# Routing statements of a three-stage kernel with one operand in a PSUM bank, rounds joined at their ends, and a new table of times for the order of its second phase

## The chip, the core and the metric

The kernel runs on one core of a Trainium2 chip. A core has five engines that work side by side, each through its own list of instructions in order: TensorE (matrix products; PE in the views, PEld for its weight loads), VectorE (DVE), ScalarE (ACT), GpSimd (POOL) and SyncE (SP, which here only issues transfers). They wait for each other through semaphores. Tiles lie in SBUF, results of TensorE in PSUM, which has eight banks; VectorE and ScalarE can reach PSUM too. The metric is the time of one execution on the device in microseconds.

## What is computed

Attention with decaying weights, then a dense layer pair, then a routed layer with eight experts. The last part is what the change touches:

```
logits = x @ w_gate                      # 4608 tokens, 8 experts
order  = argsort(-logits.flatten())      # all (token, expert) pairs, best first
for (tok, e) in order:
    if assigned[tok] >= 0 or counts[e] >= 576: continue
    assigned[tok] = e; counts[e] += 1
for e in range(8):
    h = maximum(x[assigned == e] @ w1[e], 0)      # 512 -> 1024
    out[assigned == e] = h @ w2[e]                # 1024 -> 512
```

Every expert gets exactly 576 tokens. The products are made in pieces of high and low part (three matmuls in place of one) for accuracy.

## The kernel before

`phase_ab` does the attention and the dense pair and ends at about 1042 us of the span; `phase_c` (from L711) does the routing and the experts. The greedy choice is made in eight rounds, one for each expert that fills up. `route(r)` is one round: it masks the logits (`v`), takes each token's best (`m`, `mt`), turns it into a sortable key (`n1`, `key`, `hi`), marks what each token proposes (`e0`, `m8`, `P`), and then finds the threshold at which the first expert is full by a search of six steps (two halves of three, `STEPS`). A step compares all keys with 32 or 64 thresholds (`cmp_`, 128x1152 or 128x2304 results), counts with TensorE (L865 or L869 into `pa`), masks (`ca`, L873), sums with TensorE again (L884, L885 into `pd`), and reduces to the new threshold (`dm`, `tr`, `pi`). Then come the counts (`GG`, L909), the expert that is full (`mx`, `ei`), the tokens' places (`X`, L932 and L933; `pos`, `zi`, `zl`, `zh`), the list of its tokens (`A`, `b1`, `R`, L962; `im`, `ix`, L973; `idx`, L976), and last the masks for the next round (`se`, `epen`, `tpen`, `own`, `rem`, L981 to L987). So a round is one long chain that goes to and fro between VectorE and TensorE. In rounds below `FAST` (0 and 1) GpSimd makes the differences `D` for the later steps (L833), so that their compare has one tile and a scalar.

Expert `r` needs `EI[r]` (which weights to load; SyncE) and `IDX[r]` (which rows of x to gather; GpSimd). `experts(r)` is TensorE's main work: 192 matmuls of 128x288 (L1090, first layer) and 112 of 128x512 (L1121, second layer). ScalarE and VectorE take each result over as `hh` and `hl` (L1099, L1103: three VectorE instructions for one f, a set in what follows). `split_w` makes high and low part of each weight tile, the low one on GpSimd (`w1l`, `w2l`, L1008), and `tokens` transposes the gathered rows (L1044) and splits them (`xh`, `xl`, L1046, L1047).

Each engine's order is fixed when the program is written. `route`, `weights` and `tokens` are generators that yield planned durations (`Y_TR`, `Y_Z` and the others, in us); every few matmuls `experts` calls `tick`, which moves a planned clock by `TK1` or `TK2` and lets each generator whose time has come (yield times `YS`) write its next instructions behind the matmuls written so far. A yield that is too short places a routing matmul on TensorE before its operand is ready, and as TensorE works in order, all matmuls behind it wait. Before the first expert, rounds 0 and a part of 1 run alone: `run(...)` writes round 0, a row of `WARM2` matmuls (L1147), `LEAD` = 8 pieces of round 1, then the transposes for expert 0.

Of the kernel before, what the change touches and what calls it, by code (L numbers as in the profile page):

```python
# [9 lines left out]
F32 = mybir.dt.float32  # L10
F32R = mybir.dt.float32r
# [689 lines left out]
RZ = 0.8
YS = 1.0
# [12 lines left out]
def phase_c(tc, ctx, w1, w2, rtf, rti, rth, rtb, x2d, L, out):  # L715
# [7 lines left out]
    psR = ctx.enter_context(tc.tile_pool(name="psR", bufs=2, space=PSUM))  # L723
# [41 lines left out]
    nc.gpsimd.memset(sc, 0.0)  # L765
    EI, IDX = {}, {}

    def route(r):
# [27 lines left out]
        GG = rt([128, NCOL, 2, E], BF16, "GG")
        gg = rt([128, NCOL, 2], BF16, "gg")
        if r < E - 1:

            n1 = rt([128, NCOL], I32, "n1")  # L800
            key = rt([128, NCOL], I32, "key")
            hi = rt([128, NCOL], I32, "hi")
            lo = rt([128, NCOL], I32, "lo")
            hs = rt([128, NCOL], F32, "hs")
            lf = rt([128, NCOL], F32, "lf")
            mb = mt.bitcast(I32)
            V.tensor_scalar(n1, mb, c31, c80, op0=OP.arith_shift_right, op1=OP.bitwise_or)
# [4 lines left out]
            for half in range(2):
# [6 lines left out]
                D = [None] * 3  # L819
                for s, (shift, J) in enumerate(STEPS):  # L820
                    io = F[f"s{s}"]
                    cmp_ = rt([128, NCOL, J], BF16, f"cmp{J}")
                    if s == 0:
                        V.tensor_tensor(cmp_, bc(src, 2, J), bc(io, 1, NCOL), op=OP.is_ge)
                        if fast:
                            if not half:
                                src = rt([128, NCOL], F32, "hf")
                                nc.gpsimd.tensor_copy(out=src, in_=hi)
                            for k in (1, 2):
                                D[k] = fp.tile([128, KC, CAP], F32R, tag=("xh", "xl")[k - 1], name=f"D{k}", bufs=2)  # L830
                                D[k] = D[k].rearrange("p k t -> p (k t)")[:, :NCOL * STEPS[k][1]].bitcast(F32)
                                D[k] = D[k].rearrange("p (c j) -> p c j", c=NCOL)
                                nc.gpsimd.tensor_tensor(D[k], bc(src, 2, STEPS[k][1]), bc(F[f"s{k}"], 1, NCOL),  # L833
                                                        op=OP.subtract)
                        if not half:
                            yield 1.3
# [3 lines left out]
                            V.tensor_scalar(rn[:1], rem[:1], -1.0, None, op0=OP.mult)  # L840
                            V.tensor_copy(out=rz[:1, 1, :], in_=rn[:1])
                    else:
                        if fast:
                            if s == 1:
                                V.tensor_scalar(cmp_, D[s], pi, None, op0=OP.is_ge)
                            else:
                                V.tensor_scalar(cmp_, D[s], T, pi, op0=OP.subtract, op1=OP.is_ge)
                        else:
                            thr = rt([128, J], F32, f"thr{J}")
                            if s == 1:  # L850
                                V.tensor_scalar(thr, io, pi, None, op0=OP.add)
                            else:
                                V.tensor_scalar(thr, io, T, pi, op0=OP.add, op1=OP.add)
                            V.tensor_tensor(cmp_, bc(src, 2, J), bc(thr, 1, NCOL), op=OP.is_ge)
# [378 lines left out]
```

## Time and profile before

| | |
|---|---|
| median of 3 runs | 1649.44 us (1648.26 to 1654.27) |
| the profiled execution | 1648.73 us, span 1647.0 us |
| dense phase, until about | 1042 us |
| routing before the first expert matmul | 1046.6 to about 1110 us |
| experts 0 to 5, each with a round of routing beside it | 1110 to 1533 us, 68 to 76 us each |
| experts 6 and 7, no routing left | 1533 to 1638 us |
| busy over the span | TensorE 92%, VectorE 73%, ScalarE 46%, GpSimd 37% |

How to read it: the busy shares are means over phases with different limits. In the dense phase TensorE has hardly a pause. In the expert phase it is again the engine with the most work, so what matters there is each wait of TensorE and what released it. In the stretch before the first expert nothing runs but the routing chain, so every instruction of it counts.

### The profile page before, as it was taken

Reading aid. Unit: us, or ns where it says so; the run is one execution under the profiler, and the core shown is the slowest. Engines: PE = TensorE matmul, PEld = TensorE weight load, DVE = VectorE, ACT = ScalarE, POOL = GpSimd, SP = SyncE. Lnnn points to the kernel's source line nnn. Section 1 sums busy time; section 2 is a strip of 40 time slices with the busy share of each in tenths; the row PEclk is TensorE's granted clock in tenths of the full one; section 3 lists DMA queues with packets and bytes.
Section 4 is the critical chain, followed back from the end, with each engine's and each line's share of the span. In section 5 each row is a group of like instructions: output and inputs, shape, how many; then the busy total and the mean of one; then the engine's idle time right before and its main releaser. Section 6 shows DMA issues by size and latency. Waiting matters only on the chain.

```text
span 1647.0 us, 25621 instructions
## 1 busy us (share of the span) xinstructions
PE 1508.3 (92%) x9204; PEld 1306.3 (79%) x9204; DVE 1205.0 (73%) x2743; ACT 759.4 (46%) x1581; POOL 611.3 (37%) x500
## 2 busy tenths in 40 slices
PE   6989999999999999999999999438889898898997
PEld 4778878888888888888888889328678687786986
DVE  6989965878777777777777778676777777778410
ACT  4667764555555545464545565222332232222421
POOL 4546631212121212121212122454554635546442
PEclk8889999999999999999999999759999999999999
DMA  7422221120201111111111000131332313323511
GB/s 264 153 80 77 78 104 65 39 77 21 76 29 69 39 58 39 58 47 51 58 39 58 22 20 1 34 102 44 121 115 74 125 56 121 109 74 101 172 61 36
DMA packets 48607, 122.34 MB, mean 74 GB/s; under 512 B 6624, under 2 KB 13536, under 8 KB 48224
## 3 DMA queue, kind: packets, MB, share of 16 engines
q1 hardware_dynamic: 41184, 99.80, 18.1%
q0 software_dynamic: 6144, 19.93, 3.8%
q8 instruction: 72, 1.18, 0.3%
q10 hardware_dynamic: 1152, 0.98, 0.2%
q14 instruction: 55, 0.45, 0.1%
HBM read 101.81 MB, written 18.87 MB: 73 GB/s over the span
## 4 chain that ended last, share of the span: by engine, by line
PE 72%; DVE 21%; issue 3%; ACT 2%; DMA 2%; POOL 0%; SPq 0%; ACTq 0%; POOLq 0%; DVEq 0%
PE h L394 21%; PE x L457 21%; PE ff L1090 11%; PE ff L1121 7%; PE ps L292 2%; PE ps L339 2%; PE ps L285 2%; PE ps L344 2%; DVE t L418 1%; PE tp L1044 1%; DVE work L204 1%; DVE P L794 1%; DVE t L424 1%; DVE e L790 1%; DVE work L203 1%
## 5 line engine op out<-in xcount | busy, mean ns | idle before, releaser
L438 POOL TENSOR_TENSOR gl<-t,gh 128x384 fp32r<-128x384 f32 x192 | 203.7, 1061 | 664.6 <-ACT gh L435 612.0
L394 PE MATMUL h<-xh,w0h 128*128 128x384 f32 x704 | 240.8, 342 | 3.7 <-DVE t L424 3.6
L394 PE MATMUL h<-xh,w0l 128*128 128x384 f32 x704 | 240.3, 341 | 0.0
L457 PE MATMUL x<-w1h,gh 128*128 128x512 f32 x576 | 236.3, 410 | 2.4 <-ACT gh L435 2.4
L404 ACT ACTIVATE S<-h 128x384 f32<-128x384 f32 x192 | 93.6, 487 | 307.0 <-PE h L394 306.6
L418 DVE SCALAR_TENSOR_TENSOR t<-t,S 128x384 f32<-128x384 f32 x192 | 114.9, 599 | 162.1 <-ACT t L407 161.1
L457 PE MATMUL x<-w1l,gh 128*128 128x512 f32 x576 | 230.0, 399 | 0.0
L457 PE MATMUL x<-w1h,gl 128*128 128x512 f32 x576 | 218.9, 398 | 0.4 <-POOL gl L438 0.4
L495 DVE SCALAR_TENSOR_TENSOR junk<-x2r,wg 128x512 f32<-128x512 f32 x240 | 164.2, 684 | 4.7
L394 PE MATMUL h<-xl,w0h 128*128 128x384 f32 x704 | 153.2, 340 | 0.0
L394 PEld LDWEIGHTS h<-xh,w0h 128*128 128x128 f32 x704 | 133.7, 190 | 13.4 <-DVE t L424 5.7
L1008 POOL TENSOR_TENSOR w2l<-ws,w2h 128x512 fp32r<-128x512 f32 x64 | 91.2, 1424 | 137.0 <-ACT w2h L1007 123.6
L394 PEld LDWEIGHTS h<-xh,w0l 128*128 128x128 f32 x704 | 133.6, 190 | 7.3
L1121 PE MATMUL ff<-w2h,hh 128*128 128x512 f32 x320 | 134.2, 419 | 0.0
L1121 PE MATMUL ff<-w2l,hh 128*128 128x512 f32 (+1 forms) x320 | 132.5, 414 | 0.0
L457 PEld LDWEIGHTS x<-w1h,gl 128*128 128x128 f32 x576 | 108.7, 189 | 27.4 <-POOL gl L438 1.5
L424 DVE COPY_PREDICATED t<-m,h 128x384 f32<-128x384 uint16 x192 | 114.8, 598 | 20.4 <-ACT m L413 0.7
L407 ACT ACTIVATE t<-S,bias 128x384 f32<-128x384 f32 x192 | 118.3, 616 | 19.2 <-POOL gl L438 3.3
L394 PEld LDWEIGHTS h<-xl,w0h 128*128 128x128 f32 x704 | 126.9, 189 | 0.0
L457 PEld LDWEIGHTS x<-w1h,gh 128*128 128x128 f32 x576 | 109.8, 191 | 20.9 <-ACT gh L435 3.0
L457 PEld LDWEIGHTS x<-w1l,gh 128*128 128x128 f32 x576 | 109.8, 191 | 18.0
L420 DVE TENSOR_TENSOR t<-t,h 128x384 f32<-128x384 f32 x192 | 106.3, 554 | 18.6 <-ACT T L410 0.9
(208 smaller groups left out, 3176.5 us busy)
## 6 DMA issues: line engine op xcount, KB each, us to landing
ws<-in_w SPq DMA_DIRECT2D x128, 256.0 KB, 4.1
ain<-in_qkv SPq DMA_DIRECT2D x36, 768.0 KB, 4.2
wst<-in_wio SPq DMA_DIRECT2D x32, 512.0 KB, 3.5
x2d<-x2r SPq DMA_DIRECT2D x33, 256.0 KB, 2.0
w1h<-in_qkv SPq DMA_DIRECT2D x12, 192.0 KB, 3.6
w1l<-in_qkv SPq DMA_DIRECT2D x12, 192.0 KB, 3.6
w0h<-in_qkv SPq DMA_DIRECT2D x12, 192.0 KB, 3.6
w0l<-in_qkv SPq DMA_DIRECT2D x12, 192.0 KB, 3.8
```

The costliest lines, as they stand in the source:

```text
L394: nc.tensor.matmul(h[:, :TB], w[0][f][:, hp, :], x, start=i == 0, stop=i == 11)
L404: nc.scalar.activation(S, h, AF.Square, scale=KSC)
L407: nc.scalar.activation(AT[s][2], AT[s][1], AF.Square, bias=bias[:, 0:1])
L418: nc.vector.scalar_tensor_tensor(t, t, PA - PB * PB / 4, S, op0=OP.add, op1=OP.mult)
L420: nc.vector.tensor_tensor(t, t, h, op=OP.mult)
L424: nc.vector.copy_predicated(t, m.bitcast(U16), h)
L438: nc.gpsimd.tensor_tensor(G[s][1], TT.pop(s), G[s][0].bitcast(F32), op=OP.subtract)
L457: nc.tensor.matmul(X2[n][i], g[:, i * 128:i * 128 + 128], w, start=(f == 0 and g is gh and w is wh), stop=(f == NF - 1 and g is gl))
L495: nc.vector.scalar_tensor_tensor(j, r, 1.0, wg[e // 4][:, e % 4, :], op0=OP.mult, op1=OP.mult, accum_out=L[:, c, e:e + 1])
L1008: nc.gpsimd.tensor_tensor(l, s, h.bitcast(F32), op=OP.subtract)
L1090: nc.tensor.matmul(ps[u], w[:, k, :], x[:, k, 288 * u:288 * u + 288], start=i == 0, stop=i == 11)
L1121: nc.tensor.matmul(o, h, w, start=f == 0 and i == 0, stop=f == 7 and i == len(prods) - 1, skip_group_check=t == 4)
```

## The change

Seven things are changed, all in `phase_c`.

1. A PSUM bank `st` (pool `psS`) is set aside and cut into pieces `SB[...]`. It holds `epen`, `own`, `rem`, copies of the small tables (`w8`, `s0`, `col`, `c`), and the results `m`, `key`, `n1`, `e0`, `hs`, `thr`, `gg`, `pos`, `eq`, `pa`, `zi`, `zl`, `zh`. With it every VectorE statement of `route` with two tiles has at most one of them in SBUF, and most statements with one tile read or write the bank. Nine small VectorE instructions fill it before round 0 (three of the fills stood on GpSimd).
2. The bank comes from `psR`, which has one rotating buffer in place of two; `pt` and `pc` share it.
3. `FAST` is 1: round 1 has no `D`. In round 0 `D` is made for the third step of each half alone; the second step compares against thresholds.
4. The ends of rounds overlap: `se`, `epen` and the next `v` are made behind the `X` matmuls; `tpen`, `own`, `rem` while TensorE makes the list (L962, now L989); `m`, `mt` of the next round before `idx`; the next key and first compare right behind `idx`.
5. `R[:, :, 1, :]` is made on ScalarE in all rounds (L958 is gone), and `b1` stands before `A`.
6. The yields have new values, and `YS` is 0.87 for all three generators; `RZ` is gone.
7. `LEAD` is still 8, but with fewer yields at a round's start these 8 pieces reach further: two whole steps of round 1 and the third compare.

```
-FAST = 2
+FAST = 1
-Y_TR = 1.35 ... Y_GG = 2.2, Y_X = 1.75, Y_R = 2.0, Y_Z = 1.6, Y_H = 0.35, Y_CA = 1.3, Y_IX = 1.65, RZ = 0.8, YS = 1.0
+Y_TR, Y_CA, Y_H, Y_GG, Y_X, Y_Z, Y_R, Y_IX = 2.0, 0.85, 0.5, 2.9, 2.7, 3.6, 1.3, 2.1
+YS = 0.87
...
-    psR = ctx.enter_context(tc.tile_pool(name="psR", bufs=2, space=PSUM))
+    psR = ctx.enter_context(tc.tile_pool(name="psR", bufs=1, space=PSUM))
+    psS = ctx.enter_context(tc.tile_pool(name="psS", bufs=1, space=PSUM))
...
+    bank = psS.tile([128, 512], F32, tag="st", name="st")
+    SB = {"epen": 8, "w8": 8, "s0": 32, "m": 36, "key": 36, "col": 36, "own": 36, "rem": 8, "c": 3, "e0": 288}
...
+    def best(r):
+        V.tensor_reduce(SB["m"], VN[r], axis=AX.X, op=OP.max)
+        MT[r] = rt([128, NCOL], F32, "mt")
+        V.tensor_tensor(MT[r], SB["m"], tpen, op=OP.min)
+    def keys(r):
+        n1 = SB["n1"].bitcast(I32)
+        HI[r] = rt([128, NCOL], I32, "hi")
+        mb = MT[r].bitcast(I32)
+        V.tensor_scalar(n1, mb, c31, c80, op0=OP.arith_shift_right, op1=OP.bitwise_or)
+        V.tensor_tensor(key, mb, n1, op=OP.bitwise_xor)
+        V.tensor_scalar(HI[r], key, c16, cff, op0=OP.arith_shift_right, op1=OP.bitwise_and)
+        compare0(r, HI[r])
+    def compare0(r, src):
+        CM[r] = rt([128, NCOL, 32], BF16, "cmp32")
+        V.tensor_tensor(CM[r], bc(src, 2, 32), bc(SB["s0"], 1, NCOL), op=OP.is_ge)
...
-            V.tensor_tensor(e0, v, bc(m, 2, E), op=OP.is_equal)
+            V.tensor_tensor(q0, v, bc(m, 2, E), op=OP.is_equal)
-            V.tensor_tensor(e0, e0, bc(F["w8"], 1, NCOL), op=OP.mult)
+            V.tensor_tensor(e0, q0, bc(SB["w8"], 1, NCOL), op=OP.mult)
...
         nc.tensor.matmul(pt[:, 72:], B["ones"], X72, start=True, stop=True)
         nc.tensor.matmul(pt[:, :72], B["tri"], X72, start=True, stop=True)
+        if r < E - 1:
+            V.tensor_scalar(se, SB["w8"], mx, None, op0=OP.is_equal)
+            V.scalar_tensor_tensor(epen, se, -2 * BIG, epen, op0=OP.mult, op1=OP.add)
+            V.tensor_tensor(VN[r + 1], L, bc(epen, 1, NCOL), op=OP.min)
...
+        V.tensor_tensor(b1, bc(zh, 2, 20), bc(F["i20"], 1, NCOL), op=OP.is_equal)
+        nc.scalar.activation(R[:, :, 1, :], b1, AF.Copy, scale=F["p"])
+        yield Y_Z
         V.tensor_tensor(A, bc(zl, 2, 32), bc(F["i32"], 1, NCOL), op=OP.is_equal)
-        yield 1.3
-        V.tensor_tensor(b1, bc(zh, 2, 20), bc(F["i20"], 1, NCOL), op=OP.is_equal)
-        yield 0.9
-        V.tensor_tensor(R[:, :, 0, :], b1, bc(F["col"], 2, 20), op=OP.mult)
+        yield 1.4
+        V.tensor_tensor(R[:, :, 0, :], b1, bc(SB["col"], 2, 20), op=OP.mult)
-            V.tensor_scalar(R[:, :, 1, :], b1, F["p"], None, op0=OP.mult)
```

In VectorE's order the change shows at three places. First, from the list of round 1's tokens to the proposals of round 2. Before (the last twelve here end at `mt`; the eight instructions from `n` to `P` follow):

```order
L976 TENSOR_REDUCE idx<-rt 128x5
L981 TENSOR_SCALAR se<-tf,mx 128x8
L982 SCALAR_TENSOR_TENSOR epen<-se,epen 128x8
L983 TENSOR_TENSOR tk<-gg,vd 128x36
L984 SCALAR_TENSOR_TENSOR tpen<-tk,tpen 128x36
L985 TENSOR_TENSOR m_10766<-m_10766,gg 128x36
L986 TENSOR_TENSOR own<-own,m_10766 128x36
L987 TENSOR_TENSOR rem<-rem,nn 128x8
L1129 TENSOR_TENSOR o<-ff,o 64x512
L780 TENSOR_TENSOR v<-L,epen 128x288
L782 TENSOR_REDUCE m<-v 128x36
L784 TENSOR_TENSOR mt<-m,tpen 128x36
```

After, from `m` to `P` (`st` is any piece of the bank):

```order
L788 TENSOR_REDUCE st<-v 128x36
L790 TENSOR_TENSOR mt<-st,tpen 128x36
L1012 TENSOR_REDUCE idx<-rt 128x5
L797 TENSOR_SCALAR st<-mt,ti 128x36
L798 TENSOR_TENSOR st<-mt,st 128x36
L799 TENSOR_SCALAR hi<-st,ti 128x36
L804 TENSOR_TENSOR cmp_11467<-hi,st 128x1152
L822 TENSOR_TENSOR q_11495<-v,st 128x288
L1158 TENSOR_TENSOR o<-ff,o 64x512
L824 TENSOR_TENSOR st<-q_11495,st 128x288
L826 TENSOR_REDUCE m_11496<-st 128x36
L828 TENSOR_TENSOR P<-st,m_11496 128x288
```

What stood between `idx` and `mt` has gone to places further ahead. On TensorE 40 matmuls of the second layer lie between L973 and the next L865 before, and 27 between L1007 and L892 after.

Second, from the places of the tokens to `R` in a later round, before (`hl` and `hh` are the sets of the expert):

```order
L944 TENSOR_SCALAR zl<-zi,ti 128x36
L945 TENSOR_SCALAR zh<-zi,ti 128x36
L1103 SCALAR_TENSOR_TENSOR hl<-ff,hh 128x288
L1103 SCALAR_TENSOR_TENSOR hl<-ff,hh 128x224
L1103 SCALAR_TENSOR_TENSOR hh<-ff,hh 128x64
L950 TENSOR_TENSOR A<-zl,tf 128x1152
L952 TENSOR_TENSOR b_13095<-zh,tf 128x720
L954 TENSOR_TENSOR R<-b_13095,tf 128x36x20
L958 TENSOR_SCALAR R<-b_13095,tf 128x36x20
```

And after:

```order
L976 TENSOR_SCALAR st<-st,ti 128x36
L980 TENSOR_TENSOR b_12145<-st,tf 128x720
L1132 SCALAR_TENSOR_TENSOR hl<-ff,hh 128x288
L1132 SCALAR_TENSOR_TENSOR hl<-ff,hh 128x224
L1132 SCALAR_TENSOR_TENSOR hh<-ff,hh 128x64
L983 TENSOR_TENSOR A<-st,tf 128x1152
L1132 SCALAR_TENSOR_TENSOR hl<-ff,hh 128x288
L1132 SCALAR_TENSOR_TENSOR hl<-ff,hh 128x224
L1132 SCALAR_TENSOR_TENSOR hh<-ff,hh 128x64
L985 TENSOR_TENSOR R<-b_12145,st 128x36x20
```

`A` and `b1` have changed places, `R` has one instruction fewer on VectorE, and there is one set more between them. On TensorE 4 matmuls of L1090 and 28 of L1121 lie between L933 and L962 before, and 50 of L1119 (the old L1090) between L958 and L989 after, in rounds 4 to 6; 14 and 19, or 36 and 8, in rounds 1 and 2.

Third, ahead of the first expert: the `xl` of expert 0, before,

```order
L838 TENSOR_SCALAR lo<-key,ti 128x36
L839 TENSOR_SCALAR hs<-hi 128x36
L840 TENSOR_SCALAR rn<-rem 1x8
L841 COPY rz<-rn 1x8
L1047 TENSOR_TENSOR xl_10800<-tp,xh_10799 128x4x128 x4
L1047 TENSOR_TENSOR xl_10800<-tp,xh_10799 128x4x64
L873 TENSOR_TENSOR ca<-rt,tf 128x32
```

and after:

```order
L922 SCALAR_TENSOR_TENSOR tr_10825,pi<-tr_10825,st 128x31
L884 TENSOR_SCALAR st<-tf,pi 128x64
L886 COPY T<-st 128x1
L887 TENSOR_TENSOR cmp_10832<-hi,st 128x2304
L1076 TENSOR_TENSOR xl_10838<-tp,xh_10837 128x4x128 x4
L1076 TENSOR_TENSOR xl_10838<-tp,xh_10837 128x4x64
L900 TENSOR_TENSOR ca<-rt,tf 128x32
```

They stand behind two more steps and a compare of round 1, and on TensorE the transposes stand behind those two steps' matmuls.

## Rows read from the trace of the kernel before

**Rows 1.** Windows view: us, busy us of five engines, granted TensorE clock, DMA.

```profile
core 0: us, PE busy (x) PEld busy (x) DVE busy (x) ACT busy (x) POOL busy (x), PEclk, DMA share, GB/s
1110.00:1186.00 76.00, 64.74 (x478) 55.86 (x477) 54.22 (x132) 20.66 (x43) 40.75 (x28) 0.92 0.27 85
1186.00:1533.00 347.00, 311.73 (x2150) 267.71 (x2150) 267.98 (x634) 100.39 (x210) 177.14 (x130) 0.95 0.32 102
...
1143.00:1165.00 22.00, 18.46 (x101) 14.46 (x100) 18.64 (x44) 7.59 (x14) 12.70 (x11) 1.00 0.48 156
```

**Rows 2.** Waits view, TensorE, expert phase (1110 to 1638 us): total, times, longest.

```profile
PE rt L962 <- DVE R L958: 16.9, 5, 3.6
PE rt L865 <- DVE P L794: 16.4, 5, 5.2
PE rt L932 <- DVE ei L927: 5.2, 7, 1.2
PE rt L909 <- DVE GG L905: 3.0, 2, 2.3
PE rt L962 <- ACT R L956: 1.6, 1, 1.6
PE ff L1090 <- DVE hl L1103: 1.4, 1, 1.4
PE rt L865 <- DVE cmp L845: 0.9, 1, 0.9
```

**Rows 3.** Tile view, readers of table tf: duration in ns, min/median/max.

```profile
L873 DVE TENSOR_TENSOR ca<-rt,tf x42: 168/191/193, 1057.1 to 1486.9; 128x32 f16<-128x32 f32 x42
...
L950 DVE TENSOR_TENSOR A<-zl,tf x8: 1341/1884/2461, 1084.9 to 1525.8; 128x1152 bf16<-128x1152 int32 x8
```

**Rows 4.** Timeline, VectorE and GpSimd, round 5: start, us, engine, instruction.

```profile
1425.67 1.29 POOL L1008 TENSOR_TENSOR w2l<-ws,w2h 128x512 fp32r<-128x512 f32 x1 [3.31 <-ACT w2h L1007]
...
1425.77 1.23 DVE L944 TENSOR_SCALAR zl<-zi,ti 128x36 int32<-128x36 int32 x1
...
1427.06 0.74 DVE L1103 SCALAR_TENSOR_TENSOR hl<-ff,hh 128x288 fp32r<-128x288 f32 x2
...
1427.86 2.42 DVE L950 TENSOR_TENSOR A<-zl,tf 128x1152 bf16<-128x1152 int32 x1
```

**Rows 5.** Timeline, the same engines, ahead of the first expert.

```profile
1097.99 7.73 DVE L838 TENSOR_SCALAR lo<-key,ti 128x36 int32<-128x36 int32 x1
...
1105.95 6.22 POOL L833 TENSOR_TENSOR D<-hf,tf 128x1152 f32<-128x1152 f32 x2
1106.01 1.27 DVE L1047 TENSOR_TENSOR xl<-tp,xh 128x512 fp32r<-128x512 f32 x2
```

**Rows 6.** Timeline, VectorE in round 0, on its own on the chip's critical chain.

```profile
1050.07 2.30 DVE L790 TENSOR_TENSOR e<-e,tf 128x288 f32<-128x288 f32 x1
...
1052.89 3.74 DVE L794 TENSOR_TENSOR P<-e,m 128x288 bf16<-128x288 f32 x1
...
1068.90 4.50 DVE L845 TENSOR_SCALAR cmp<-D,pi 128x1152 bf16<-128x1152 f32 x1
...
1083.11 0.30 DVE L936 TENSOR_TENSOR_SCAN sc<-one,rt 128x72 f32<-128x72 f32 x1 [0.27 <-PE rt L932]
...
1087.06 0.91 DVE L954 TENSOR_TENSOR R<-b,tf 128x720 bf16<-128x720 bf16 x1
...
1091.37 0.17 DVE L976 TENSOR_REDUCE idx<-rt 128x5 int32<-128x10 f32 x1 [0.34 <-PE rt L973]
```

**Rows 7.** Timeline, VectorE, round 1 with GpSimd at rest.

```profile
1093.75 0.52 DVE L807 TENSOR_SCALAR n<-mt,ti 128x36 int32<-128x36 int32 x1
...
1097.61 0.46 DVE L794 TENSOR_TENSOR P<-e,m 128x288 bf16<-128x288 f32 x1
```

**Rows 8.** Chain that ended last, the last two experts: start, us, what.

```profile
1561.11 25.49 PE ff L1121 x112
1586.60 25.58 PE ff L1090 x192
```

More of the change, by code (lines that the diff above doesn't have):

```diff
@@ L746, in ps_r @@
         return psR.tile([128, 512], F32, tag="rt", name="rt")[:, :n]
+    bank = psS.tile([128, 512], F32, tag="st", name="st")
+    SB = {"epen": 8, "w8": 8, "s0": 32, "m": 36, "key": 36, "col": 36, "own": 36, "rem": 8, "c": 3, "e0": 288}
+    at = 0
+    for k, n in SB.items():
+        SB[k] = bank[:, at:at + n]
+        at += n
+    at = 0
+    for k, n in {"thr": 64, "hs": 36, "gg": 72, "pos": 72, "eq": 36}.items():
+        SB[k] = SB["e0"][:, at:at + n]
+        at += n
+    SB["n1"] = SB["thr"][:, :36]
+    SB["zi"], SB["pa"] = SB["thr"][:, :36], SB["hs"]
+    SB["zl"], SB["zh"] = SB["eq"], SB["pos"][:, 36:]
+    epen, own, rem = SB["epen"], SB["own"], SB["rem"]
     tpen = kp.tile([128, NCOL], F32, name="tpen")
-    epen = kp.tile([128, E], F32, name="epen")
-    rem = kp.tile([128, E], F32, name="rem")
-    own = kp.tile([128, NCOL], F32, name="own")
     rn = kp.tile([128, E], F16, name="rn")
@@ L765, in phase_c @@
     nc.gpsimd.memset(sc, 0.0)
-    EI, IDX = {}, {}
+    V.memset(epen, BIG)
+    V.memset(own, 0.0)
+    V.memset(rem, float(CAP))
+    for k in ("w8", "s0", "col"):
+        V.tensor_copy(out=SB[k], in_=F[k])
+    for i, (shift, _) in enumerate(STEPS):
+        V.memset(SB["c"][:, i:i + 1], float(1 << shift))
+    EI, IDX = {}, {}
+    VN, MT, HI, CM = {0: L}, {}, {}, {}
+    key = SB["key"].bitcast(I32)
+    def best(r):
[13 more added lines that the diff above has]
+        V.tensor_tensor(CM[r], bc(src, 2, 32), bc(SB["s0"], 1, NCOL), op=OP.is_ge)
     def route(r):
         fast = r < FAST
-        v = rt([128, NCOL, E], F32, "v")
-        m = rt([128, NCOL], F32, "m")
-        e0 = rt([128, NCOL, E], F32, "e0")
+        q0 = rt([128, NCOL, E], F32, "q0")
+        e0 = SB["e0"].rearrange("p (c e) -> p c e", e=E)
         m8 = rt([128, NCOL], F32, "m8")
@@ L839, in route @@
                             V.tensor_scalar(hs, hi, 65536.0, None, op0=OP.mult)
-                            V.tensor_scalar(rn[:1], rem[:1], -1.0, None, op0=OP.mult)
-                            V.tensor_copy(out=rz[:1, 1, :], in_=rn[:1])
-                    else:
[L843 to L854, printed above, removed]
+                            places()
+                    elif s == 2 and fast:
+                        cmp_ = rt([128, NCOL, J], BF16, "cmp64")
+                        V.tensor_scalar(cmp_, D, T, pi, op0=OP.subtract, op1=OP.is_ge)
+                        T2 = rt([128, 1], F32, "T")
+                        V.tensor_tensor(T2, T, pi, op=OP.add)
+                        T = T2
+                    else:
+                        cmp_ = rt([128, NCOL, J], BF16, f"cmp{J}")
+                        thr = SB["thr"][:, :J]
@@ L862, in route @@
+                            T = rt([128, 1], F32, "T")
+                            V.tensor_copy(out=T, in_=thr[:, :1])
+                        V.tensor_tensor(cmp_, bc(src, 2, J), bc(thr, 1, NCOL), op=OP.is_ge)
+                    yield (1.4 if half == 0 and s == 0 else Y_TR + 1.3 * J / 32) + Y_H * (half == 1 and s == 0)
                     pa = ps_r(32)
@@ L900, in route @@
             yield from proposals()
-            V.tensor_scalar(rn[:1], rem[:1], -1.0, None, op0=OP.mult)
-            V.tensor_copy(out=rz[:1, 1, :], in_=rn[:1])
+            places()
             for a in range(2):
@@ L1053, in each @@
             for d in f(r):
[L1054 removed]
+                yield d
     threads = [[0.0, each(f)] for f in (route, weights, tokens)]
```

132 lines of the change are left out of this document (53 added, 79 removed).

## The prediction

> **What bounds the kernel now.** I read the windows first. In the expert phase TensorE is busy for 311.7 of 347 us and VectorE for 268.0 [rows 1], so TensorE is the bound there and what it does not work is what can be won. [...] Then the waits of TensorE [rows 2]: 45.4 us in all, and nearly all of it at two places of a round, the list (behind `R`, 16.9 + 1.6) and the proposals (behind `P`, 16.4 + 0.9); the rest stands at `ei` (5.2), `GG` (3.0) and `hl` (1.4). All of these are released by VectorE but one. Then I asked the timeline why VectorE is late. `zl`, 36 columns, takes 1.23 us and ends with GpSimd's `w2l`, and `A` takes 2.42 [rows 4] where its fastest takes 1.34 [rows 3]; `lo`, 36 columns again, takes 7.73 us [rows 5]. Both operands of `zl` and of `A` lie in SBUF. Statements with one operand in PSUM do not show this: `xl` runs within GpSimd's 6.22 us `D` at 1.27 us for two [rows 5], and `ca` is 168 to 193 ns in all 42 places [rows 3]. Before the first expert the chain stands alone, and there blocked statements are time of the kernel: `e` 2.30, `P` 3.74, `cmp` 4.50 [rows 6].
>
> The sum starts from the profiled execution, 1648.7 us, which is 0.7 below the median. The matmuls of the experts do not change: the last two experts show 112 of L1121 in 25.49 us and 192 of L1090 in 25.58, so 0.228 and 0.133 us each [rows 8]. I use these prices as TensorE's cover.
>
> **Change, before the first expert.** In round 0 `P` should take 0.46 as in round 1 beside a resting GpSimd [rows 7], which is −3.3; `e` has the same 288 columns, so −1.8. The second step's `cmp` no longer waits for GpSimd's difference: 4.50 becomes a threshold and a compare of 1152 columns, some 0.3 + 1.34 [rows 3], −2.9; in the other half, where `D` came in time, the threshold and dearer compare cost about +0.8. Added are nine small fills at 0.15 or so (as `idx`, 0.17 [rows 6]), +1.4; `se`, `epen`, `v` ahead of the scan, 0.6; `m` and `mt` ahead of `idx`, 0.3. That is −4.9 at `idx`. From `idx` (1091.37 [rows 6]) to the first `xl` (1106.01 [rows 5]) there are 14.6 us, 7.7 of them `lo`. After, the chain from `n` to `P` is 4.3 long [rows 7], some 0.7 of `lo` to `rz` follow, then two steps are put ahead of the transposes. A step is a compare of 1.34, `ca` 0.19, some 1.2 in five or six small statements, and two trips over TensorE of about 0.5, by the 0.27 and 0.34 that `sc` and `idx` waited [rows 6]; behind the second stands a compare of 2304 columns, at 2.7. Together 4.3 + 0.7 + 3.7 + 5.1 = 13.8, so −0.8. Bounds: −7.7 if all this is hidden by the gather, +3 if the transposes of expert 0, which stand behind those matmuls, come late. I take **−6** for the stretch, between −12 and −1.
>
> **Change, TensorE's waits.** At the proposals 27 matmuls of L1121 stand between the last routing product of a round and L892: 27 × 0.228 = 6.15 us. VectorE has 4.3 from `n` to `P` [rows 7] to do in that time, at times an `o` of about 0.7 among it, and the first compare is among it now. Before, 40 × 0.228 = 9.1 us stood against a longer and blocked chain. No wait: −17. At the list 50 matmuls of L1119, 50 × 0.133 = 6.65 us, lie between the product of `X` and L989. VectorE's work from `X` on is `ei` 0.2; `se`, `epen`, `v` 0.9; the undisturbed stretch from `sc` to the end of `R`, 1083.11 to 1087.97, 4.86 [rows 6]; and three sets at 0.80 [rows 4], 8.4 in all. `X` is ready some 0.6 before TensorE gets there, so a wait of about 1.15 in rounds 2 to 4 and 0.4 to 0.8 in the others, together about 6 where 18.5 were. `R`'s second half on ScalarE ends earlier and costs nothing while ScalarE, busy 100.4 of 347 us [rows 1], is free; without that cover it is the 1.6 of [rows 2]. At `ei`, `GG` and `hl` I expect nothing; for places that are close (third compares, an `o` or `xl` at the queue's head) I add 4. So 45.4 becomes 10: **−35.4**, between −28 and −42. VectorE's queue behind `A` and `R` holds the sets of the expert, which TensorE needs a few matmuls later; with waits near 1 us the four result banks cover it. One rotating bank in place of two in `psR` costs nothing I can see: each group of TensorE already waits for VectorE's reading of the one before. Round 1 without `D` pays two dearer compares of 2304 columns, one ahead of the first expert (counted), one beside expert 0.
>
> **Change, price of a PSUM operand.** From [rows 4] a set of three instructions with 576 columns takes 0.80, from [rows 5] two with 1,024 take 1.27: that is 1.15 ns a column and 0.05 us an instruction, while `P` [rows 7], with all in SBUF, has 288 columns in 0.46, more than that. So I put it at nothing, and bound it from above in the rival below.
>
> [...]
>
> **Change, clock.** [...] From 1143 to 1165 the clock is 1.00 [rows 1] though TensorE is busy only 18.5 of 22 us, with the waits of 1.6 us (behind ScalarE's `R`) and about 1 us in or beside it; the long waits, up to 3.6 and 5.2 us, head [rows 2] and lie elsewhere. With waits near 1 us I expect most to return: **−16**, between 0 and −20.
>
> 1648.7 − 6 − 35.4 − 16 = **1591**.
>
> **Rivals.** *The waits go and the clock stays low.* That would hold if the clock fell for another reason than these waits, say the mix of matmuls at an expert's boundary. For it: the waits stand at the same places of every round as the boundaries, so that the trace cannot separate them. Against: the row at clock 1.00. Price: the 16, so about 1607.
>
> *It doesn't do what it says.* VectorE would stay blocked by GpSimd with one operand in PSUM. Then list and proposals keep their 3.3 us per round [rows 2], round 0 keeps its blocked statements, the clock stays, and only the small waits at `ei` and `GG` and the earlier `se` remain as a gain, some 5 us: about 1644. Against it `xl` within `D` and the even `ca` [rows 3, 5].
>
> *The bank makes wide statements slower* (the slower side). Six compares, `A`, `b1`, `R`, the two on 288 columns and `GG` with their like have about 13,250 columns a round with an operand in the bank, most read again and again through a broadcast, which none of `ca`, `hl`, `xl` does over so many columns. Were a column twice as dear (1.15 ns more), that is 15.2 us of VectorE a round; VectorE's idle 23% [rows 1] is scattered, and I let it take 5. Then TensorE waits 10 more in each of 6.5 rounds, 65; round 0 is 15 longer; the clock stays low, 16: 1591 + 96, about 1687. By the same sum the gain is used up at about 0.75 ns more a column.
>
> **How the numbers follow.** The forecast, 1591, has 0.78, with an own range of 1577 to 1603 (the start between −12 and −1, the waits left 4 to 17, the clock within some 6). The clock rival at 1607 has 0.13, no effect at 1644 has 0.04, slower at 1687 has 0.05. The range from 1577 to 1613 takes in the forecast and the clock rival with their bounds and leaves out about 2 in 10, at either end and in the two others. About 0.5%, some 8 us, is what a measurement of this kernel can tell from no change: faster 0.91, same 0.04 (the rival at 1644), slower 0.05.
>
> **What would show it.** Right: in the profile after, VectorE's 36-column statements stay below 0.3 us whatever GpSimd does, and `A` below 1.5; the first expert matmul comes some 6 us earlier; TensorE's wait at the proposals is gone and one of about 1 us stands at L989 in each round; the granted clock of experts 0 to 5 is 0.98 or more. Wrong: clock of 0.95 with few waits (the clock rival); `P`, `A` or `zl` still ending with an instruction of GpSimd (no effect); compares and `A` of 2 us and more that no GpSimd instruction explains (the bank's price). A long wait at the transposes L1073 or at the gather would be a step that I left out, since the time between `idx` and them is shorter than before.

## The result

The changed kernel takes 1597.84 us (median; 1595.46 to 1598.85), the kernel before 1649.28: a ratio of 0.968 with a 95% interval of 0.9658 to 0.9703, so 51 us less. The profiled execution is 1598.85 us with a span of 1597.1, 49.9 below the one of before. Forecast were 1591 in a range of 1577 to 1613. The time and the three terms of its sum came out near what was said. What the experiments then showed is that the first two parts of the change (the bank and what it needs) give more than the whole gain by themselves, and that the other five together cost about 18 us of it.

The windows of the changed kernel, in the columns of [rows 1]:

```profile
1104.00:1180.00 76.00, 72.79 (x545) 63.56 (x544) 51.37 (x153) 24.43 (x52) 32.45 (x28) 0.96 0.28 93
1180.00:1500.00 320.00, 305.71 (x2178) 265.01 (x2177) 210.14 (x625) 107.94 (x227) 157.42 (x138) 0.99 0.37 118
```

TensorE is busy for 306 of 320 us where it was for 312 of 347, at a clock of 0.99 in place of 0.95, and VectorE has 66% in place of 77%: its statements became shorter. TensorE's waits in the expert phase (1106 to 1590 us; what waits, what for, us in total, times, longest), against [rows 2]:

```profile
PE ff L1119 <- DVE hl L1132: 7.7, 9, 2.0
PE rt L989 <- DVE R L985: 6.4, 5, 2.7
PE tp L1073 <- DMA xg<-x2d,idx: 0.9, 1, 0.9
PE ff L1150 <- DVE hl L1132: 0.6, 1, 0.6
```

These are 15.6 us in place of 45.4. The proposals (L892) are gone from the list, `ei` and `GG` too. The list of tokens (L989) has 6.4 for 18.5. New at the head stands `hl`, which had 1.4: the first matmul of a new f waits for VectorE to empty a result bank.

The statements that were held, in the view of one line (count, then ns min/median/max, answering [rows 3]):

```profile
L983 DVE TENSOR_TENSOR A<-st,tf x8: 1347/1348/1349, 1082.5 to 1463.5; 128x1152 bf16<-128x1152 int32 x8
L942 DVE SCALAR_TENSOR_TENSOR fw<-nn,st x8: 161/162/164, 1077.2 to 1453.2; 128x8 f32<-128x8 f32 x8
```

`A` took up to 2461 ns before and is now the same in all eight rounds. So the 49.9 us split as follows. The first expert matmul starts 4.0 us earlier (TensorE's timeline of the changed kernel, then of the one before; start, us):

```profile
1106.07 0.59 PE L1119 MATMUL ff<-xh,w1h 128*128 128x288 f32 x1
```

```profile
1110.03 0.59 PE L1090 MATMUL ff<-xh,w1h 128*128 128x288 f32 x1
```

TensorE's waits behind it: 45.4 − 15.6 = 29.8. What is left, 49.9 − 4.0 − 29.8 = 16.1 us, is put down to the granted clock, 0.96 and 0.99 in the two stretches that had 0.92 and 0.95 [rows 1]; as a remainder it also holds whatever the other two terms miss.

### The profile page after: what moved, and what is told of

It reads as the page before. It is cut to its first block, busy times and chain, and to the rows that moved or that the text cites. A ratio compares the mean times of both kernels' runs of the same rounds, so it can differ in the third digit from the quotient of the medians.

```text
span 1597.1 us, 25569 instructions
## 1 busy us (share of the span) xinstructions
PE 1495.5 (94%) x9180; PEld 1296.0 (81%) x9180; DVE 1128.8 (71%) x2766; ACT 761.4 (48%) x1587; POOL 561.0 (35%) x490
## 4 chain that ended last, share of the span: by engine, by line
PE 76%; DVE 14%; DMA 3%; ACT 2%; issue 2%; POOL 1%; SPq 0%; ACTq 0%; POOLq 0%; DVEq 0%
PE h L394 22%; PE x L457 22%; PE ff L1150 10%; PE ff L1119 10%; PE ps L292 2%; PE ps L339 2%; PE ps L344 2%; PE ps L285 2%; DVE t L418 1%; DVE cmp L887 1%; DMA wst<-in_wio 1%; PE tp L1073 1%; DVE t L424 1%; DVE work L204 1%; DVE t L420 1%
## 5 line engine op out<-in xcount | busy, mean ns | idle before, releaser
L394 PEld LDWEIGHTS h<-xh,w0h 128*128 128x128 f32 x704 | 134.0, 190 | 13.2 <-DVE t L424 5.4
L1037 POOL TENSOR_TENSOR w2l<-ws,w2h 128x512 fp32r<-128x512 f32 x64 | 82.4, 1290 | 160.9 <-ACT w2h L1036 160.7
L424 DVE COPY_PREDICATED t<-m,h 128x384 f32<-128x384 uint16 x192 | 114.8, 598 | 20.4 <-ACT m L413 0.7
L1150 PE MATMUL ff<-w2h,hh 128*128 128x512 f32 x320 | 127.9, 400 | 0.6 <-DVE hl L1132 0.6
L1150 PE MATMUL ff<-w2l,hh 128*128 128x512 f32 (+1 forms) x320 | 127.9, 400 | 0.0
L1119 PE MATMUL ff<-xh,w1h 128*128 128x288 f32 x512 | 117.1, 306 | 9.0 <-DVE hl L1132 7.7
```

The source lines that it names most:

```text
L394: nc.tensor.matmul(h[:, :TB], w[0][f][:, hp, :], x, start=i == 0, stop=i == 11)
L424: nc.vector.copy_predicated(t, m.bitcast(U16), h)
L1037: nc.gpsimd.tensor_tensor(l, s, h.bitcast(F32), op=OP.subtract)
L1119: nc.tensor.matmul(ps[u], w[:, k, :], x[:, k, 288 * u:288 * u + 288], start=i == 0, stop=i == 11)
L1150: nc.tensor.matmul(o, h, w, start=f == 0 and i == 0, stop=f == 7 and i == len(prods) - 1, skip_group_check=t == 4)
```

## The experiments

| kernel | us | ratio to before (95%) |
|---|---|---|
| changed kernel | 1597.8 | 0.968 (0.966 to 0.970) |
| bank in SBUF | 1655.9 | 1.004 (1.002 to 1.005) |
| R later on ScalarE | 1586.3 | 0.961 (0.959 to 0.963) |
| R on VectorE | 1589.8 | 0.964 (0.962 to 0.966) |
| 4 pieces ahead | 1598.7 | 0.969 (0.967 to 0.971) |
| R later, 4 pieces | 1589.9 | 0.963 (0.961 to 0.964) |
| R later, 4 pieces, w1h later | 1590.7 | 0.964 (0.962 to 0.966) |
| R later, 6 pieces | 1586.2 | 0.961 (0.959 to 0.963) |
| P later by 5.1 us | 1625.6 | 0.985 (0.983 to 0.986) |
| P later by 2.5 us | 1603.7 | 0.972 (0.971 to 0.974) |
| ends apart | 1600.1 | 0.969 (0.968 to 0.971) |
| before, times 15% longer | 1643.5 | 0.996 (0.995 to 0.998) |
| before, with the bank alone | 1579.5 | 0.957 (0.956 to 0.958) |

**Is it the PSUM operand?** The changed kernel with the same bank in SBUF.

```
-    bank = psS.tile([128, 512], F32, tag="st", name="st")
+    bank = kp.tile([128, 512], F32, name="st")
```

> The changed kernel with one edit: the bank is a tile in SBUF, not in PSUM; order, yields and everything else stay. Theory (the gain comes from VectorE no longer being held by GpSimd): statements of VectorE with both tiles in SBUF take 2 us and more beside GpSimd's w1l and w2l again, TensorE waits 30 us or more in the expert phase in place of 15.6, the clock falls below 0.98 again, round 0 is some 5 us longer: 1625 to 1645 us. Rival (the new order and the new times alone made the gain): 1595 to 1605 us, with no statement of 36 columns above 0.5 us at the places where TensorE waits.

It took 1655.9 us, more than the theory asked for (1625 to 1645) and 0.4% more than the kernel before. Waits of TensorE are back behind `R` (10.8), `P` (6.5), `hl` (11.4), compares and others. The same lines in the same view, then one of the places on the timeline of VectorE and GpSimd:

```profile
L983 DVE TENSOR_TENSOR A<-st,tf x8: 1346/1348/4160, 1086.0 to 1515.4; 128x1152 bf16<-128x1152 int32 x8
L942 DVE SCALAR_TENSOR_TENSOR fw<-nn,st x8: 167/168/5361, 1081.2 to 1501.3; 128x8 f32<-128x8 f32 x8
```

```profile
1501.30 5.36 DVE L942 SCALAR_TENSOR_TENSOR fw<-nn,st 128x8 f32<-128x8 f32 x1
...
1501.66 1.31 POOL L1037 TENSOR_TENSOR w2l<-ws,w2h 128x512 fp32r<-128x512 f32 x1
1502.91 3.72 POOL L1037 TENSOR_TENSOR w1l<-ws,w1h 128x512 fp32r<-128x512 f32 x3
```

`fw`, eight columns, takes 5.36 us through a `w2l` and three `w1l` of GpSimd, and ends at 1506.66, where the last of them ends at 1506.63. Undisturbed it takes 168 ns with both tiles in SBUF and 162 with one in PSUM, and `A` 1348 both ways. So the operand in PSUM frees the statement and costs these two nothing. Clearly dearer are only the thresholds, which write to the bank: 254 ns in place of 241 (32 columns) and 348 in place of 315 (64).

**Who makes `hl` late?** The timeline of the changed kernel in round 4, on three engines, shows it:

```profile
1320.21 0.91 DVE L980 TENSOR_TENSOR b<-st,tf 128x720 bf16<-128x720 int32 x1
...
1321.15 0.89 ACT L981 ACTIVATE R<-b,tf 128x720 bf16<-128x720 bf16 x1 [6.80 <-DVE b L980]
1321.95 0.69 ACT L1128 ACTIVATE hh<-ff 128x288 fp32r<-128x288 f32 x2
...
1322.38 0.76 DVE L1132 SCALAR_TENSOR_TENSOR hl<-ff,hh 128x288 fp32r<-128x288 f32 x2 [1.26 <-ACT hh L1128]
...
1322.89 0.90 PE L1119 MATMUL ff<-xh,w1h 128*128 128x288 f32 x2 [1.99 <-DVE hl L1132]
```

ScalarE has nothing to do and stands 6.80 us at `R` until `b` is there. `hh` of the expert is next in its list, `hl` on VectorE waits for `hh`, and TensorE 1.99 us for `hl`. `A` stands behind that `hl`, so that the list is late too. The waits of ScalarE from 1107 to 1500 us have it in one row:

```profile
ACT R L981 <- DVE b L980: 30.6, 7, 6.8
```

The edit puts `R` behind the yield, some 3 us later in the list:

```
-        nc.scalar.activation(R[:, :, 1, :], b1, AF.Copy, scale=F["p"])
         yield Y_Z
+        nc.scalar.activation(R[:, :, 1, :], b1, AF.Copy, scale=F["p"])
```

> The changed kernel with one edit: ScalarE's second half of R is written behind the yield Y_Z, so about 3 us later in ScalarE's list. Theory (ScalarE stands for 5 to 7 us at this instruction because it waits for b1, and the hh of the expert behind it come late, so TensorE waits for hl and A is late too): waits of TensorE behind hl fall from 8.3 us to 3 or less, the list's from 6.4 to 3, the time from 1598 to 1589 to 1594 us. Rival (hl is late because of VectorE's own queue, a 2304-column compare ahead of it): waits behind hl stay at 7 to 8 us, 1597 to 1599 us.

It took 1586.3 us, better than the theory's 1589 to 1594. ScalarE's row, then TensorE's waits:

```profile
ACT R L982 <- DVE b L980: 3.6, 5, 1.5
```

```profile
PE ff L1119 <- DVE hl L1132: 4.8, 7, 1.6
PE rt L989 <- DVE R L985: 1.4, 3, 0.7
```

The list lost 5.0 us of wait and `hl` 3.5. The rival has a part in what is left: ahead of the longest of the waits left, 1.61 us at 1300.35, VectorE runs a compare of 2304 columns from 1297.39 (2.54 us), and the set of `hl` stands behind it. The wait of 0.80 us at 1241.44 stands behind such a compare too, and those of 0.82 and 0.63 us behind `b`.

To give the instruction back to VectorE is the other way out:

```
-        nc.scalar.activation(R[:, :, 1, :], b1, AF.Copy, scale=F["p"])
...
+        if r:
+            V.tensor_scalar(R[:, :, 1, :], b1, F["p"], None, op0=OP.mult)
...
```

> The changed kernel with one edit: the second half of R goes back to VectorE behind the first (from round 1 on), as in the kernel before. Theory (the instruction on ScalarE holds up hh): the waits behind hl fall as in the run with R later, but VectorE's chain to the list is longer by one instruction of up to 0.9 us in each round, so the list's wait grows from 6.4 to about 9 us: 1594 to 1599 us. Rival (handing this work to ScalarE is worth what it takes off VectorE's chain): list waits of 12 us, waits behind hl unchanged, 1603 to 1606 us.

It took 1589.8 us: `hl` has 4.9, much as in the run before, and the list 5.0, where the theory had 9 and the rival 12. The hold on ScalarE cost more than the whole instruction does on VectorE. The fifth part of the change is a loss where it was put.

**Can the start come earlier?** In the changed kernel the transposes of expert 0 and `xl` stand behind two steps and a compare of round 1.

```
-LEAD = 8
+LEAD = 4
```

> The changed kernel with one edit: 4 pieces of round 1 in place of 8 are written ahead of the transposes of expert 0, so the transposes stand ahead of the two steps of round 1 and xl ahead of the compare with 2304 columns. Theory (these steps hold the transposes up by 4 us): the first expert matmul comes 3 to 5 us earlier, the two steps go beside expert 0 for nothing: 1593 to 1595 us. Rival (the gather or the clock, which is low until some microseconds into expert 0, sets the start anyway): 1597 to 1599 us.

The first expert matmul came at 1097.90, 8 us earlier, and the time is 1598.7: the rival's number, but not by its reasons, since the start did move and the clock is 1.00 from 1097 to 1120. With `R` later as well:

> Two edits of the earlier runs together: the second half of R later in ScalarE's list, and 4 pieces of round 1 ahead of the transposes. With 4 pieces alone the first expert matmul came at 1097.90 in place of 1106.07, and beside experts 0 and 1 it was all given back: a wait of 3.2 us at the list of round 1, some 4 us behind hl and the second layer's operands, a granted clock of 0.93 to 0.96 from 1120 to 1185. Theory (what was given back came from the same late hh and the waits that it made): list wait of round 1 below 1.5 us, clock 0.99 there, 1578 to 1582 us. Rival (with the start earlier the supply of weights or the shorter way of round 1 sets experts 0 and 1): 1585 to 1587 us, with waits that name w2h, w2l or xg.

It took 1589.9 us, where 8 pieces gave 1586.3. Where the 8 us went (timeline of ScalarE, VectorE and TensorE, then the window behind it):

```profile
1142.31 1.28 ACT L1036 ACTIVATE w1h<-ws 128x512 fp32r<-128x512 f32 x2 [5.90 <-DMA ws<-in_w]
...
1146.26 0.68 DVE L1158 TENSOR_TENSOR o<-ff,o 64x512 f32<-64x512 f32 x1 [3.97 <-ACT o L1157]
1146.87 1.34 DVE L983 TENSOR_TENSOR A<-st,tf 128x1152 bf16<-128x1152 int32 x1
...
1149.08 1.38 PE L989 MATMUL rt<-R,A 128*128 128x160 bf16 x9 [3.74 <-DVE R L985]
```

```profile
1150.00:1160.00 10.00, 10.00 (x41) 7.82 (x40) 5.94 (x18) 0.83 (x2) 8.41 (x9) 0.76 0.25 78
```

Round 1 is later against expert 0, its weights arrive late, and `w1h`, which nobody needs yet, waits for them at the head of ScalarE's list; `o` behind it, VectorE's `o`, `A` and the list follow. So I took that hold away:

```
         load_w1(r)
+        if r == 1:
+            yield 8.0
```

> The run with R later and 4 pieces ahead, with one more edit: ScalarE's w1h of expert 1 are written 8 planned us later. In that run the start came 8 us earlier, and then w1h of expert 1 stood 5.9 us at the head of ScalarE's list waiting for its weights, o behind it, VectorE's o 3.97 us behind that, A and R behind that, TensorE 3.74 us at the list of round 1, and the granted clock was 0.76 to 0.91 from 1150 to 1180. Theory (one waiting instruction at the head of ScalarE's list made the whole chain): list wait of round 1 below 1 us, clock 0.98 or more in 1150 to 1180, 1578 to 1583 us. Rival (the supply of weights itself is too late when the start is earlier): TensorE waits for the first layer's operands of expert 1, 1586 to 1590 us.

The list's wait fell from 3.74 to nothing in round 1, and the time stayed: 1590.7. In its place stands the next thing that is late, the rows of x for expert 1:

```profile
PE tp L1075 <- DMA xg<-x2d,idx: 7.2, 4, 3.0
```

So the theory that one hold made it all is wrong (it asked for 1578 to 1583 us), and the rival named the wrong supply (weights in place of tokens). `idx` of round 1 comes at 1148.55, and at 1146.88 with `R` later and 8 pieces: expert 0 ends earlier, round 1 does not, and the transposes of expert 1 stand too close behind it. Six pieces:

> R later, and 6 pieces of round 1 ahead of the transposes in place of 8 or 4. Theory (the earlier start is worth what it gains as long as round 1 is not so late that w1h of expert 1 waits at the head of ScalarE's list): start 2 to 5 us earlier than with 8, list wait of round 1 below 2 us, 1581 to 1585 us. Rival (any earlier start is given back at the supply of expert 1): 1586 to 1590 us.

It took 1586.2 us against 1586.3 with eight: the start came at 1097.70, and it is not seen in the time. TensorE waits 6.7 us for `hl` in place of 4.8 and 1.6 for the list of round 1. The traces say where it goes: expert 1 begins at 1162.52 in place of 1169.85, and expert 2 at 1228.01 in place of 1230.01, so 5 us are lost within expert 1. Waits explain some 2 of them; for the rest I have no cause to name.

**Do the waits cost clock?** Two useless compares of 2304 columns ahead of `P` in rounds 2 to 6, then one.

```
...
+            if 1 < r < E - 1:
+                for _ in range(2):
+                    V.tensor_tensor(junk, bc(hi, 2, 64), bc(F["s2"], 1, NCOL), op=OP.is_ge)
             V.tensor_tensor(P, e0, bc(m8, 2, E), op=OP.is_equal)
```

> The changed kernel with two added VectorE compares of 2304 columns (2.55 us each, their result is not used) ahead of P in rounds 2 to 6, so that TensorE waits at the proposals again: about 4 us in each of five rounds, 20 in all. Theory (the waits pulled the granted clock down before, and the change got that back): beside the 20 us the clock from 1180 to 1500 falls from 0.99 to 0.95 to 0.97, low stretches right behind these waits, 1623 to 1632 us. Rival (the clock in the kernel before fell for another reason): clock 0.99 as in the changed kernel, 1616 to 1620 us.

> The same with one such compare (2.55 us) in each of rounds 2 to 6: waits of about 1.5 us at five places, 7.5 in all. Theory (long waits pull the clock down, waits near 1.5 us do not): clock from 1180 to 1500 stays at 0.99, 1604 to 1607 us. Rival (every wait costs clock in proportion): clock 0.97 to 0.98, 1608 to 1612 us.

TensorE's waits at the proposals, then the window 1180 to 1500 us that both expectations name, of the run with two:

```profile
PE rt L896 <- DVE P L832: 20.4, 5, 5.3
```

```profile
1180.00:1500.00 320.00, 291.53 (x2046) 249.51 (x2046) 226.79 (x626) 100.16 (x211) 163.78 (x130) 0.96 0.35 109
```

And of the run with one:

```profile
PE rt L896 <- DVE P L832: 6.5, 5, 1.8
```

```profile
1180.00:1500.00 320.00, 301.45 (x2126) 259.12 (x2125) 216.84 (x617) 104.88 (x221) 163.61 (x135) 0.98 0.37 116
```

Five waits of 2.9 to 5.3 us, 20.4 in all, make the kernel 27.8 us longer, and the clock falls to 0.96 where the changed kernel has 0.99. Five of 0.3 to 1.8, 6.5 in all, make it 5.9 longer, no more than the waits themselves, at 0.98. The theory of the first run holds: the long waits took the clock along, and the matmuls around them are the same ones. That of the second holds in the main only: it asked for 0.99 and 1604 to 1607 us, and the run has 0.98 and 1603.7, so short waits are not shown to be wholly free.

**What do the joined ends bring?** `se`, `epen`, `v`, `tpen`, `own`, `rem`, `m`, `mt` back behind `idx`.

```
+            V.tensor_scalar(se, SB["w8"], mx, None, op0=OP.is_equal)
+            V.scalar_tensor_tensor(epen, se, -2 * BIG, epen, op0=OP.mult, op1=OP.add)
...
             best(r + 1)
             if r + 1 < E - 1:
```

> The changed kernel with its fourth part undone: se, epen, v, tpen, own, rem, m, mt stand behind idx again, as before; bank, yields and the rest stay. Theory (joining the ends shortens the way from the list to the proposals): the way from idx to P grows by ten instructions, some 2.6 us, past the cover of 27 matmuls (6.15 us), so TensorE waits 1.5 to 2.5 us at the proposals in six rounds, and the list's wait falls by up to 0.9 us in each: 1600 to 1612 us. Rival (with the bank alone the chain is short enough, and joining only matters before the first expert, some 1 us): 1597 to 1600 us.

It took 1600.1 us, where the two ranges meet. The waits at the proposals are there as the theory says, but small (3.9 us, four times), and the interval overlaps that of the changed kernel. So joining the ends brings about 2 us, if anything.

**Would longer times have done?** The kernel before with every planned duration 15% longer.

```
-YS = 1.0
+YS = 1.15
```

> The kernel before with one edit: all planned durations 15% longer (YS 1.15), so that TensorE has more matmuls between the routing products. Theory (VectorE's statements are held by GpSimd at places no table can name, 2 to 7 us at a time): waits fall from 45 us to 25 to 35, clock below 0.98, 1628 to 1645 us. Rival (the times were simply too short, and longer ones would have done without the bank): waits below 15 us, 1595 to 1615 us.

It took 1643.5 us, and 34 us of waits are left, as the theory says, but not where it says. At the routing places they fell to some 10 us:

```profile
PE tp L1044 <- DMA xg<-x2d,idx: 18.9, 17, 2.3
PE ff L1090 <- DVE hl L1103: 5.6, 3, 3.7
PE rt L865 <- DVE cmp L845: 2.7, 1, 2.7
PE rt L962 <- ACT R L956: 2.3, 1, 2.3
PE rt L865 <- DVE P L794: 1.6, 3, 1.0
```

But a round now ends so late that the transposes wait 17 times for the gathered rows. With this one value of `YS` the places are right for the list and too late for the gather; no other value was run, so a better table for the old kernel is not excluded. The clock stayed at 0.93 to 1186 and 0.96 to 1533 us, close to [rows 1].

**And the bank without the rest?** The kernel before with the first two parts alone: bank, fills, one buffer in `psR` and the few statements rewritten for it (among them `T`, `rz` and the two halves of `pos`); order, yields, `FAST`, `LEAD` and `R` as before.

```
-        m = rt([128, NCOL], F32, "m")
+        m = SB["m"]
...
-            V.tensor_tensor(e0, e0, bc(F["w8"], 1, NCOL), op=OP.mult)
+            V.tensor_tensor(e0, q0, bc(SB["w8"], 1, NCOL), op=OP.mult)
...
-        V.tensor_tensor(R[:, :, 0, :], b1, bc(F["col"], 2, 20), op=OP.mult)
+        V.tensor_tensor(R[:, :, 0, :], b1, bc(SB["col"], 2, 20), op=OP.mult)
```

> The kernel before with the bank alone (first and second part of the change, with the fills and one buffer in psR): order of the statements, yields, FAST, LEAD and the place of R are those of before. Theory (the bank is nearly the whole gain, order and times only follow from it): with undisturbed statements the old places are wide enough (40 matmuls of 0.228 us, 9.1 us, at the proposals against some 7 us of VectorE), waits of TensorE 10 to 20 us, clock 0.98 to 0.99, 1595 to 1606 us; round 0 keeps its 4.5 us behind the difference. It also has no R on ScalarE, so it may come out below the changed kernel. Rival (bank and new places need each other): waits of 25 us and more, 1615 to 1635 us.

It took 1579.5 us, 0.957 of the kernel before: the fastest of all, 18 us below the changed kernel, with intervals far apart. This kernel with its bank in SBUF was not run, so that the 70 us are the PSUM operand's, and not the rewriting's, is argued from the run with the bank in SBUF above. Its waits of TensorE from 1100 to 1590 us, its window and its first expert matmul:

```profile
PE rt L888 <- DVE cmp L865: 4.3, 1, 4.3
PE rt L985 <- ACT R L979: 1.8, 1, 1.8
PE tp L1067 <- DMA xg<-x2d,idx: 1.1, 1, 1.1
PE ff L1113 <- DVE hl L1126: 0.6, 1, 0.6
PE rt L955 <- DVE ei L950: 0.4, 1, 0.4
```

```profile
1180.00:1500.00 320.00, 318.85 (x2327) 281.67 (x2326) 226.09 (x655) 114.00 (x240) 170.75 (x147) 1.00 0.38 123
```

```profile
1099.96 0.59 PE L1113 MATMUL ff<-xh,w1h 128*128 128x288 f32 x1
```

From 1200 us on TensorE does not wait for the routing at all: 318.9 busy of 320, and 1.1 us of wait for gathered rows. Of the 8.2 us of waits, 6.1 stand in round 1, behind the difference `D` of the old `FAST` = 2 and `R` on ScalarE in that round. The compare with `D` is itself worth a look (tile view of this run; ns min/median/max):

```profile
L865 DVE TENSOR_SCALAR cmp<-D,pi x4: 1755/2898/4635, 1055.4 to 1127.1; 128x1152 bf16<-128x1152 f32 x4
```

It has one tile in SBUF and a scalar, no second tile. In the kernel before one of its four took 0.82 us at 1058.51, with GpSimd at rest. Here the longest, at 1105.39, takes 4.63 while GpSimd makes the second `D`, and ends at 1110.02, 0.62 us behind it; the other three end 0.62 us behind such an instruction too. So the bank does not free every statement: this one is still held by GpSimd, and it is the third part of the change that takes it out.

Parts three to seven (`FAST`, ends, `R` on ScalarE, times, further-reaching pieces) together took back 18 us. 11.6 of them are the place of `R` (the run with `R` later). The earlier start is not the other 7, though the first expert matmul comes 6.1 us earlier here than in the changed kernel. By the first matmul of expert 1 that is gone (the changed kernel, then the bank alone):

```profile
1170.82 0.42 PE L1119 MATMUL ff<-xh,w1h 128*128 128x288 f32 x2
```

```profile
1172.01 0.42 PE L1113 MATMUL ff<-xh,w1h 128*128 128x288 f32 x2
```

The gain is made behind it, in experts 1 to 5 (the stretch from there to the first matmul of expert 6, in the columns of [rows 1]: the changed kernel, `R` later, the bank alone):

```profile
1170.82:1485.04 314.22, 299.93 (x2148) 259.02 (x2147) 211.95 (x632) 105.08 (x220) 155.49 (x135) 0.99 0.37 118
1169.85:1474.43 304.58, 297.59 (x2147) 257.66 (x2146) 211.24 (x632) 106.03 (x220) 155.77 (x135) 0.99 0.38 122
1172.01:1463.57 291.56, 290.40 (x2149) 255.06 (x2148) 221.65 (x640) 100.25 (x210) 150.71 (x130) 1.00 0.38 122
```

For almost the same number of matmuls these take 314, 305 and 292 us. TensorE waits 13.2, 6.1 and 1.1 us in them and is busy for 300, 298 and 290. So what the kernel with `R` later still loses against the old order lies there, 5.0 us of it in small waits and 7.2 in matmul time (some 2 of these are 16 transposes that the kernel with the bank alone makes in expert 6). Which part brings that, the order, the times or `R` on ScalarE, no run separates; the new table's shorter ways are what I suspect, and it stays open.

## Why the prediction was right, and where it was not

- **What bounds the kernel**: TensorE with its waits, and VectorE held by GpSimd as their cause. The run with the bank in SBUF, where holds, waits and time all come back, confirms it.
- **Before the first expert, −6**: measured −4.0. The routing started later in this execution, in code that the change does not touch: the last copy of `L` is at 1048.07 where it was at 1046.40 (between 1045.24 and 1048.61 in all fourteen profiles). Counted from there it is −5.6, all of it up to `idx` (forecast −4.9); from `idx` to the first matmul both take 18.66 us (forecast −0.8). The held `lo` went, and two steps and a compare took its place; that they do so to the hundredth is chance. The 4.50 us of `cmp` [rows 6] were not a wait for GpSimd's difference, as the sum says, but the hold shown above for the compare with `D`; its term stays the same.

VectorE's timeline at the two ends, in the changed kernel and, for the first, in the kernel before:

```profile
1048.07 0.17 DVE L508 COPY L<-tp 128x8 f32<-128x8 f32 x1 [0.73 <-PE tp L506]
...
1087.41 0.16 DVE L1012 TENSOR_REDUCE idx<-rt 128x5 int32<-128x10 f32 x1
```

```profile
1046.40 0.17 DVE L508 COPY L<-tp 128x8 f32<-128x8 f32 x1 [0.73 <-PE tp L506]
```

- **TensorE's waits, −35.4**: measured −29.8. Proposals, `ei`, `GG`: nothing, as said. The list: 6.4 where 6 were said, but not as 1.15 in rounds 2 to 4; it is 0.3 to 2.7 in five rounds, and 5.0 of the 6.4 went when `R` was moved, so they came from ScalarE's hold. The step that failed is the sentence that `R`'s second half on ScalarE "costs nothing" while ScalarE is free. It was free by its busy time (29% [rows 1]) and not by its order: an instruction that waits 6.8 us stops all behind it. I had asked that question of VectorE's queue and not of ScalarE's. The hold made these 5.0 us and 3.5 of the 8.3 at `hl`, where nothing was expected; the other 4.8 at `hl` stayed with `R` later, and they alone are more than the 4 that the sum had for all close places.
- **Price of the PSUM operand, nothing**: right, but for 13 and 33 ns in the thresholds.
- **Clock, −16**: no run shows the 16 us as a term of its own; they were my estimate. What the traces show in its place: behind the 5.24 us for which TensorE waits for `P` in the kernel before, up to 1173.50, the granted clock is 0.50 from 1171 to 1177 and matmuls of L1121 start every 0.43 us; ahead of that wait, at 1.00, they start every 0.23 (below). By the windows 0.08 × 76 + 0.05 × 347 = 23.4 us were short of a clock of 1.00 before [rows 1] and 0.04 × 76 + 0.01 × 320 = 6.2 after, idle time among them, so an estimate of 17. In the sum 16.1 is what is left. In experts 1 to 5 the matmuls are busy for 299.9 us (the first of the three rows above) in place of 311.7 ([rows 1], 1186 to 1533 us), so about 12 of it are read directly. The run with the long waits ahead of `P` shows the cause: it lost 7.4 us beyond the 20.4 that were added. In that proportion 29.8 us would bring 11, an estimate. So the cause is right, and that the remainder meets the forecast to a tenth is luck.

The clock of the kernel before ahead of that wait and behind its start, in the columns of [rows 1], then TensorE's timeline:

```profile
1165.00:1168.00 3.00, 3.00 (x15) 2.37 (x13) 2.86 (x5) 0.60 (x1) 2.54 (x3) 1.00 0.27 55
1171.00:1177.00 6.00, 3.50 (x19) 3.02 (x20) 3.74 (x8) 0.60 (x1) 4.09 (x4) 0.50 0.45 141
```

```profile
1167.64 0.39 PE L1121 MATMUL ff<-w2l,hh 128*128 128x512 f32 x1
1167.87 0.39 PE L1121 MATMUL ff<-w2h,hh 128*128 128x512 f32 x1
1173.50 0.42 PE L865 MATMUL rt<-P,cmp 128*128 128x32 bf16 x9 [5.24 <-DVE P L794]
...
1175.50 0.63 PE L1121 MATMUL ff<-w2h,hh 128*128 128x512 f32 x1
1175.93 0.63 PE L1121 MATMUL ff<-w2h,hl 128*128 128x512 f32 x1
```

- **Rivals**: the clock did not stay low (0.99); VectorE is no longer held; no wide statement is slower (compare 1355 ns, `A` 1348, where [rows 3] have 1341 at best).
- **What the sum did not ask**: what each part is worth alone. I set the new places (27 and 50 matmuls) against the undisturbed chain and booked −17 and −12 to "the change". The old places against the same chain, 40 matmuls of L1121 at the proposals, 9.1 us against the 6.7 from `idx` to the end of `P` [rows 6, 7], would have suggested that the bank needs no other part.

## What to carry to other kernels

Where a vector instruction of eight columns takes microseconds and ends with an instruction of GpSimd, as `fw` did with 5.36 us, try an operand in PSUM: with it `fw` took 0.16 here, and one bank, with its fills and the few statements rewritten for it, was worth 70 us of 1650, and no table of times was touched. When such a hold is gone, time the kernel with the old order first; the tables and moves that were made around it have to earn their place again. Before work is handed to an engine because it is idle, look at what stands behind the instruction in that engine's list and how long it will wait at the head, which was up to 6.80 us for `R` here.

## What the runs showed of the hardware that was not expected

- A hold of VectorE did not scale with its own work: with the bank in SBUF a statement of eight columns and 0.17 us took 5.36, through four instructions of GpSimd one after another.
- TensorE paid for long waits a second time: 20.4 us of added waits of 2.9 to 5.3 us cost 27.8 us with the clock at 0.96, while 6.5 us of waits up to 1.8 us cost 5.9 with the clock at 0.98; without either it is 0.99.
- A statement with one tile in SBUF and a scalar was held too: the compare with `D` took 1.76 to 4.63 us in the run with the bank alone, and 0.82 beside a resting GpSimd in the kernel before.
